# Fewer, wider idle matmuls between the stages, and H's tables loaded one page of x earlier

## The chip, the cores and the metric

The kernel runs on one core of a Trainium2 chip. The metric is the device time of one execution in microseconds (us). The kernel before takes 1393.24 us, the median of three runs (1391.94 to 1394.51).

## The reference

Three stages stand one behind the other. First the real part of a two-dimensional Fourier transform of x (8 x 3072 x 256), over the sequence and over the features. Then a mixture of experts with soft slots, and then a feed-forward layer with a squared rectifier:

```python
X = fft(fft(x, axis=1), axis=2).real.reshape(24576, 256)
logits = X @ phi                                  # 24576 x 32
d = exp(logits - logits.max(0)); d /= d.sum(0) + 1e-9
slot_input = (d.T @ X).reshape(8, 4, 256)
slot_out[e] = relu(slot_input[e] @ w1[e]) @ w2[e]  # e = 0..7
c = exp(logits - logits.max(1)); c /= c.sum(1) + 1e-9
Y = c @ slot_out
h = relu(Y @ w_in)
out = (s * h * h + b) @ w_out                      # 24576 x 256
```

## The kernel before, in words

The Fourier transform is never formed for all features. Because the logits are X @ phi, the features' transform is folded into phi (`project`, L480), and each batch of x is multiplied by that small matrix. The sequence of 3072 is split as 24 times 128.

**Stage V and T (to about 87 us).** 24 pages of x, 1 MB each, are loaded in turned form (`load_x`, L286). `emit_v` (L396) multiplies a part of a batch by the projected phi, `turn_v` transposes the result, and `emit_t` (L437) does the transform over 128 points into the table `tt`. The last batch is done in two pieces, `tpa` in a buffer with the tag "vq" and `tpb` in one with the tag "vt". Each tag has two buffers of PSUM, which the tiles take in turn. ScalarE copies `tpa` (L446) and VectorE copies `tpb` (L459) into `tt`.

**Logits (about 87 to 97 us).** The loop at L576 makes 16 blocks of logits, `lp` (L584), with 256 matmul instructions. ScalarE copies each into the pages `lg` (L597), and VectorE takes the maximum of each over its entries (L599). The maxima are joined into `cm1` (L606).

**The global maximum (to about 104.5 us).** `cm1` is transposed by TensorE (`mt`, L612), reduced by VectorE (L617), put on a diagonal (`dg`, L619), spread over all partitions by a product with ones (`mb`, L621), and copied to `cmb` (L622). Between the transpose and the reduction the program calls the remaining steps of the side work on the weights of the last layer (`side_step`, L614), which include VectorE's L216.

**H (to about 121 us).** The loop at L661 subtracts `cmb` from the logits (`emit_d`, on VectorE and POOL in turn, L647), takes exponentials on ScalarE (L683), and multiplies by the tables of H (L666). The two tables are loaded by `htab_load` (L349), which also clears parts of them on POOL. After the loads have landed, `htab_clear` (L358) moves and clears further parts on POOL.

**Sums, experts and last layer.** From 121 to about 180 us `r_sum` (L734) forms d.T @ x from 24 pages of x in a second layout (`load_xr`, L325), while the weights of the experts are loaded behind them. The experts follow. From about 230 us to the end the last layer runs; its matmuls (L1165, L1168, L1135) make up most of the time.

**Idle matmuls.** `keep_warm(t, k)` (L187) issues k matmuls of a matrix of ones into a PSUM tile that nobody reads. It is called ahead of `project` (L493), behind T (L533, four calls), and three times behind the logits (L610, L613, L624). A product of f32 operands is issued as two passes, so one call of `nc.tensor.matmul` gives two weight loads and two matmul instructions.

**What sets the order.** The instructions of each engine run in the order in which the program is written. All large loads are issued on SP's queue. While V runs, the letters of `ORDER` (L297) say which load comes next: x a page of x in turned form, w a part of w_out, s and l the tables of the logits, r a page of x in the second layout, h a table of H. `pump_a` takes the next letter when a page is free and the planner's clocks allow it, and L515 takes what is left. A load takes a page from a ring of 15. Pages of x that `ORDER` did not load are put at the head of the list `todo` (L564), whose entries are issued when pages come free.

Of the kernel before, what the change touches and what calls it, by code (L numbers as in the profile page):

```python
# [8 lines left out]
F32 = mybir.dt.float32  # L9
# [23 lines left out]
def tile_fft2__then__softmoe__then__act_relu2(  # L33
# [18 lines left out]
    nc = tc.nc  # L52
    P = 128
    NS1 = 24
    B, S, D = 8, NS1 * P, xp.shape[-1]
    NE = phi.shape[1]
    NG = B // 2
    M = 2 * NS1
    R = P // 2 + M
# [25 lines left out]
    ones = const.tile([P, P], F32, name="ones")  # L85
    dd = const.tile([P, 2, 2, D], F32, name="dd")
# [9 lines left out]
    def page(shape, dt, name, among=9):  # L96
        k = next(k for k, p in enumerate(pools[:among]) if p[2] < p[1])
        pools[k][2] += 1
        return pools[k][0].tile(shape, dt, tag="page", name=name), k
# [4 lines left out]
    def drop(k):  # L104
        pools[k][2] -= 1
# [5 lines left out]
    def dma_ready(cost=2.57):  # L111

        at["dma"] = max(at["dma"], at["pe"] - 1.0) + cost
        return at["dma"] + 1.3

    def busy(eng, cost, after=0.0):
        at[eng] = max(at[eng], after, at["pe"]) + cost
# [69 lines left out]
    def keep_warm(t, k):  # L187

        for _ in range(k):
            nc.tensor.matmul(t, lhsT=ones[:, :t.shape[0]], rhs=ones[:, :t.shape[1]], start=True, stop=True)  # L190

    def wo_load(k):
        if k % 2 == 0:
            t, kk = page([P, 8, D], F32, "wo")
            wo.append(t)
            wok.append(kk)
            whl.append(page([P, 8, 2, D], F16, "whl")[0])
        w = wo[k // 2][:, 4 * (k % 2):4 * (k % 2) + 4, :]
        hl = whl[k // 2][:, 4 * (k % 2):4 * (k % 2) + 4]
        d = w.rearrange("p k d -> p (k d)")  # L200
        top, inv = wsc[:, 0, 2 * k:2 * k + 2], wsc[:, 1, 2 * k:2 * k + 2]

        def scale():
            nc.vector.tensor_scalar(out=top, in0=top, scalar1=1e-30, scalar2=1.0 / WMAX, op0=ALU.max, op1=ALU.mult)
            nc.vector.reciprocal(inv, top)
            if k < 3:
                cast()

        def cast():
            for j in range(2):  # L210
                busy("act", 0.62)
                nc.scalar.activation(out=hl[:, 2 * j:2 * j + 2, 0, :], in_=w[:, 2 * j:2 * j + 2], func=AF.Copy,
                                     scale=inv[:, j:j + 1])

        def low(j):
            nc.vector.scalar_tensor_tensor(out=hl[:, 2 * j:2 * j + 2, 1, :], in0=w[:, 2 * j:2 * j + 2], scalar=inv[:, j:j + 1],  # L216
                                           in1=hl[:, 2 * j:2 * j + 2, 0, :], op0=ALU.mult, op1=ALU.subtract)
            if j and k % 2:
                drop(wok[k // 2])

        steps = double_steps(d, w_out.rearrange("(k p) d -> p k d", p=P)[:, 4 * k:4 * k + 4, :], False)
        steps.append((0.0, lambda: nc.vector.tensor_reduce(
            out=top, in_=d.rearrange("p (a n) -> p a n", a=2), axis=AX.X, op=ALU.max, apply_absolute_value=True), 1.15))
        steps.append((0.0, lambda: bias_add(k, d.rearrange("p (k d) -> p k d", d=D)), 0.0))
        steps.append((0.0, scale, 0.35))
        if k == 3:
            steps.append((0.0, cast, 0.0))
        steps += [(0.0, lambda j=j: low(j), 0.65) for j in range(2)]
        side_at[k] = dma_ready()
        side_work.extend((k, *f) for f in steps)  # L230
# [42 lines left out]
    def bias_add(k, d):  # L273

        for i in range(0 if k else 1, 4):
            nc.gpsimd.tensor_tensor(out=bias, in0=bias if k or i > 1 else d[:, 0], in1=d[:, i], op=ALU.add)
# [15 lines left out]

    NX = 3 * B
    CR = 1.5
    WARM = 4
    LEAD, TOL, LT, LX, HX = 14.0, 0.5, 0, 0, 1
    ORDER = "xxxwxxxxxxwxxxxxxwxxxxwxsrllrrrhh"  # L297
    tpool = tc.alloc_tile_pool(name="tpool", bufs=1)
    doubles += [((3, 1, 3, 1)[k], lambda k=k: wo_load(k)) for k in range(4)]

    order = list(ORDER)

# [78 lines left out]
    with tc.tile_pool(name="xtp", bufs=1, side="right") as xtp, tc.tile_pool(name="vp", bufs=1, side="right") as vp, \  # L381
# [108 lines left out]
                nc.vector.tensor_copy(phd[:, :, sg], pp.rearrange("p c j e -> p c (j e)"))  # L490
            nc.vector.tensor_scalar(out=phd[:, :, 1, NE:], in0=pp[:, :, 1], scalar1=-1.0, scalar2=None, op0=ALU.mult)

        keep_warm(psv.tile([P, 4 * P], F32, tag="vt", name="warm", bufs=2)[:, :P], 18)  # L493
        project()

        def step_v(n):
# [33 lines left out]
        side_step(0.0, True)  # L530
        nc.sync.dma_start(out=sb_in[:, 0:1], in_=sb_d[0].partition_broadcast(P))
        nc.sync.dma_start(out=sb_in[:, 1:2], in_=sb_d[1].partition_broadcast(P))
        keep_warm(psv.tile([P, 4 * P], F32, tag="vt", name="warm", bufs=2)[:, :P], WARM)  # L533
        for i in range(2):
            htab_clear(i)

# [35 lines left out]
    with tc.tile_pool(name="ps_l", bufs=6, space=PSUM) as psl, \  # L572
            tc.tile_pool(name="ps_m", bufs=1, space=PSUM) as psm:
        mxp[:] = [psm, 1]
        done_l = 0
        for st in range(NCH // 2):  # L576
            halves = [(h, (st + 4 * h) % 8) for h in range(2)]
            lps = {h: psl.tile([R, KC, NG * NE], F32, name="lp") for h, _ in halves}
            for k in range(2 * KC):
                q = P // 2 * (k % 2)  # L580
                m = M if q else P // 2
                for h, i8 in halves:
                    r = slice(64 * h, 64 * h + 64)
                    nc.tensor.matmul(  # L584
                        lps[h][q:q + m, k // 2, :], lhsT=ltabs[st // 4][0][r, 2 * KC * (i8 % 4) + k, 0:m],
                        rhs=tt[r, 2 * KC * i8 + k].rearrange("p b e -> p (b e)"), start=True, stop=True,
                        tile_position=(64 * h, q), skip_group_check=True,
                    )
            for h, i8 in halves:
                if h and st % 4 == 3:  # L590
                    drop(ltabs[st // 4][1])
                lp = lps[h]
                busy("dve", 0.55)
                at["pe"] += 1.06
                dst = lg[i8 // 2][:, 8 * (i8 % 2) + h:8 * (i8 % 2) + 8:2].rearrange("p k g e -> p k (g e)")
                if done_l < NCH - 1:
                    nc.scalar.copy(dst, lp)  # L597
                lv = lp.rearrange("p k (b e) -> p (k b) e", e=NE)
                nc.vector.tensor_reduce(out=cm[:, done_l, :], in_=lv.rearrange("p k e -> p e k"), axis=AX.X, op=ALU.max)  # L599
                if done_l == NCH - 1:  # L600
                    nc.scalar.copy(dst, lp)
                if done_l == NCH - 4:
                    nc.vector.tensor_reduce(out=cm[:, NCH, :], in_=cm[:, :NCH - 4, :].rearrange("p i e -> p e i"), axis=AX.X,
                                            op=ALU.max)
                if done_l == NCH - 1:
                    nc.vector.tensor_reduce(out=cm1, in_=cm[:, NCH - 4:, :].rearrange("p i e -> p e i"), axis=AX.X,  # L606
                                            op=ALU.max)
                done_l += 1
        warm = psl.tile([R, 2, B * NE], F32, name="lp")[:, 0, :R]
        keep_warm(warm, 8)  # L610
        mt = psm.tile([NE, R], F32, tag="mt", name="mt")
        nc.tensor.transpose(mt, cm1, ident[:R, :R])  # L612
        keep_warm(warm, 3)  # L613
        while side_step(0.0, True):  # L614
            pass
        cm2 = temps.tile([NE, 1], F32, name="cm2", bufs=1)
        nc.vector.tensor_reduce(out=cm2, in_=mt, axis=AX.X, op=ALU.max)  # L617
        dg = temps.tile([NE, NE], F32, name="dg", bufs=1)
        nc.vector.tensor_scalar(out=dg, in0=ident[:NE, :NE], scalar1=cm2, scalar2=None, op0=ALU.mult)  # L619
        mb = psm.tile([P, NE], F32, tag="mt", name="mb")  # L620
        nc.tensor.matmul(mb, lhsT=ones[:NE, :], rhs=dg, start=True, stop=True)  # L621
        nc.vector.tensor_copy(cmb, mb)  # L622
        mxp[0] = None
        keep_warm(warm, 8)  # L624
        fill_stack()

    temps.release()
# [10 lines left out]
    with tc.tile_pool(name="ps_h", bufs=3, space=PSUM) as psh:  # L638
# [22 lines left out]
        for i in range(-3, NCH + 1):  # L661
            if 0 <= i < NCH:
                dt = dts.pop(i)
                hp = [psh.tile([P, 2, 8 * MH], F32, name=f"hp{q}") for q in range(2)]
                for k, q in [(0, 0), (1, 0), (0, 1), (1, 1)] if i == NCH - 1 else [(0, 0), (0, 1), (1, 0), (1, 1)]:
                    nc.tensor.matmul(  # L666
                        hp[q][:, k, :], start=True, stop=True,
                        lhsT=dt.rearrange("p k g e -> p (k g e)")[:, 128 * (2 * k + q):128 * (2 * k + q) + 128],
                        rhs=htabs[i // 8][0][:, 2 * (i % 8) + k].rearrange("p q m -> p (q m)"),
# [231 lines left out]
    warm = pst.tile([P, 2, 2, P], F32, tag="htp_", name="warm")[:, 0, 0, :]  # L901
    sip = psa.tile([P, 2, NE], F32, tag="dps", name="sip")
    for c in range(2):
        for n, (j, k) in enumerate([(0, 0), (0, 1), (1, 0), (1, 1)]):
            nc.tensor.matmul(
                sip[:, c, :], lhsT=dd[:, j, k, c * P:(c + 1) * P], rhs=rt[:, k, 32 * j:32 * j + 32],
                start=(n == 0), stop=(n == 3),
# [144 lines left out]
    for _ in range(2):  # L1052
        p = pools.pop()
        assert p[2] == 0
        p[0].release()
    with tc.tile_pool(name="fr", bufs=4) as frp, tc.tile_pool(name="fo", bufs=3) as fo, \
# [134 lines left out]
        while len(seq) < 3 * NFC * NBLK:  # L1191
# [3 lines left out]
            t = min(may, key=lambda t: (done[t] + (t - 1) * lag, t))  # L1195
# [10 lines left out]
        for u, (n, f, t) in enumerate(seq):  # L1206
# [8 lines left out]
            if w % 6 == 3 and w < 36 and m % 4 == 3:  # L1215
                k = w // 6
# [107 lines left out]
```

## Time and profile before

| | us |
|---|---|
| median of three runs | 1393.24 |
| lowest and highest run | 1391.94, 1394.51 |
| the profiled execution's own time | 1392.02 |
| its span, first to last instruction | 1390.1 |
| TensorE busy, matmuls | 1370.7 |
| VectorE busy | 1169.2 |
| ScalarE busy | 1008.2 |

PE is TensorE, and PEld its weight loads, which run beside its matmuls. DVE is VectorE, ACT ScalarE, POOL GpSimd. SP issues transfers. A line such as L584 is a line of the kernel, and a line of a helper such as L190 stands for every call of it. In a chain of waits each piece is what the next one waited for; "issue" is time in which an engine waited for nothing that the profile shows. The queue "q1" carries the kernel's transfers, and "instruction" queues carry the engines' code.

### The profile page before, as it was taken

The numbers are of one execution on the slowest core, as the hardware profiler recorded it, in microseconds if no ns is written. First come the engines' busy times: TensorE is split into PE (matmuls) and PEld (weight loads), VectorE is DVE, ScalarE is ACT, GpSimd is POOL, SyncE is SP. The second block draws the span as 40 slices with busy tenths as digits, with TensorE's granted clock in tenths as the row PEclk, the third lists the DMA queues.
The fourth block names the chain that finished last, engine by engine and source line by source line (L and its number), as shares of the span: only waits on it lengthen the run. The fifth ranks groups of instructions, "written<-read, shape, count | busy, mean of one in ns | idle before, by whom it ended". The sixth has DMA issues, their size and how long they took to land.

```text
span 1390.1 us, 23074 instructions
## 1 busy us (share of the span) xinstructions
PE 1370.7 (99%) x9026; PEld 839.0 (60%) x9026; DVE 1169.2 (84%) x1490; ACT 1008.2 (73%) x1423; POOL 235.9 (17%) x286
## 2 busy tenths in 40 slices
PE   8989999999999999999999999999999999999998
PEld 6767555666666666666666666666666666666665
DVE  2577737998989898989898998989898989888886
ACT  2776126777778787777787777777777777777775
POOL 1057000121212121212121211111111111111110
PEclk9999999999999999999999999999999999999999
DMA  9997990101010101010102011010101010101000
GB/s 383 414 368 299 393 409 21 40 21 36 23 37 24 37 20 37 20 37 24 34 22 37 23 30 31 19 37 22 35 24 36 21 37 24 38 23 33 24 21 29
DMA packets 72733, 112.68 MB, mean 81 GB/s; under 512 B 34112, under 2 KB 59968, under 8 KB 65200
## 3 DMA queue, kind: packets, MB, share of 16 engines
q1 hardware_dynamic: 72592, 111.18, 23.7%
q8 instruction: 71, 1.16, 0.3%
q14 instruction: 38, 0.31, 0.1%
q0 software_dynamic: 32, 0.03, 0.0%
HBM read 78.89 MB, written 26.21 MB: 76 GB/s over the span
## 4 chain that ended last, share of the span: by engine, by line
PE 89%; DMA 2%; DVE 1%; issue 1%; ACT 0%; SPq 0%; DVEq 0%; ACTq 0%
PE op L1165 47%; PE op L1168 24%; PE fhp L1135 12%; PE racc L741 3%; DMA w2t<-in_moe_w_dram 2%; PE hp L666 1%; PE dps L726 1%; SPq L1098 0%; PE lp L190 0%; DVE cm L599 0%; DVE r L1141 0%; DVE rhl L1126 0%; PE eop L971 0%; PE lp L584 0%; PE gp L1069 0%
## 5 line engine op out<-in xcount | busy, mean ns | idle before, releaser
L1165 PE MATMUL op<-whl,rhl 128*128 128x512 f16 x3072 | 1025.3, 379 | 0.8 <-ACT rhl L1125 0.6
L1168 PE MATMUL op<-whl,rhl 128*128 128x256 f16 x3072 | 835.7, 273 | 0.0
L1140 ACT ACTIVATE r<-fhp,wsc 128x768 f32<-128x768 f32 (+1 forms) x513 | 461.9, 900 | 230.1 <-PE fhp L1135 229.1
L1141 DVE SCALAR_TENSOR_TENSOR r<-fhp,r 128x768 f32<-128x768 f32 (+1 forms) x513 | 488.6, 953 | 114.8 <-ACT r L1140 105.0
L1126 DVE TENSOR_TENSOR rhl<-r,rhl 128x768 f16<-128x768 f32 x511 | 505.5, 989 | 0.9 <-ACT rhl L1125 0.9
L1165 PEld LDWEIGHTS <-rhl 128*128 128x128 f16 x3072 | 300.5, 98 | 335.5 <-ACT rhl L1125 0.9
L1125 ACT CAST rhl<-r 128x768 f16<-128x768 f32 x511 | 420.0, 822 | 1.8 <-DVE r L1141 1.8
L1168 PEld LDWEIGHTS <-rhl 128*128 128x128 f16 x3072 | 300.6, 98 | 62.6 <-issue 0.3
L1180 POOL TENSOR_TENSOR ot<-ot,bias 128x256 f32<-128x256 f32 x189 | 138.9, 735 | 972.6 <-DVE ot L1178 972.6
L1135 PE MATMUL fhp<-ct,g 128*128 128x384 f16 x1024 | 250.4, 326 | 1.1 <-DMA g<-gs 0.9
L1135 PEld LDWEIGHTS <-g 128*128 128x128 f16 x1024 | 99.9, 98 | 69.0 <-issue 1.5
L1177 ACT ACTIVATE o<-op,small 128x256 f32<-128x256 f32 x189 | 90.0, 477 | 16.6 <-PE op L1168 16.6
L1178 DVE SCALAR_TENSOR_TENSOR ot<-op,small,o 128x256 f32<-128x256 f32 x192 | 91.5, 477 | 0.3
L408 PE MATMUL vt<-xb,phd 128*64 128x384 f32 (+3 forms) x288 | 48.7, 479 | 3.1 <-DMA xb<-in_x_turned_dram 2.7
L741 PE MATMUL racc<-xrt,dh 128*64 128x256 f32 x384 | 44.5, 383 | 0.4 <-DVE dh L731 0.4
L408 PEld LDWEIGHTS vt<-xb,phd 128*64 128x64 f32 x288 | 27.2, 139 | 21.9 <-issue 10.0
L741 PEld LDWEIGHTS racc<-xrt,dh 128*64 128x64 f32 x384 | 26.3, 137 | 20.9 <-issue 4.5
L478 ACT COPY tt<-tps 32x512 f32<-32x512 f32 x48 | 27.7, 577 | 5.1 <-PE tps L464 4.6
L420 ACT COPY vts<-vt 128x512 f32<-128x512 f32 (+1 forms) x16 | 8.5, 533 | 28.1 <-PE vt L408 27.9
L433 DVE COPY v<-vq 128x512 f32<-128x512 f32 (+1 forms) x15 | 8.3, 592 | 24.2 <-PE vq L429 24.2
L788 POOL TENSOR_TENSOR lg<-lg,rm 112x512 f32<-112x512 f32 x16 | 22.5, 1409 | 4.1 <-DVE rm L786 4.1
L770 POOL TENSOR_TENSOR lg<-et,lg 112x512 f16<-112x512 f32 x16 | 18.6, 1162 | 0.0
(228 smaller groups left out, 494.2 us busy)
## 6 DMA issues: line engine op xcount, KB each, us to landing
xb<-in_x_turned_dram SPq DMA_DIRECT2D x24, 1024.0 KB, 20.1
xrt<-in_x_pages_dram SPq DMA_DIRECT2D x24, 1024.0 KB, 12.5
out_dram<-ot SPq DMA_DIRECT2D x128, 128.0 KB, 1.7
w1t<-in_moe_w_dram SPq DMA_DIRECT2D x8, 1024.0 KB, 13.7
out_dram<-ot SPq DMA_DIRECT2D x128, 64.0 KB, 2.0
raw<-in_moe_w_out_dram SPq DMA_DIRECT2D x4, 1024.0 KB, 20.3
raw<-in_moe_w_in_dram SPq DMA_DIRECT2D x4, 1024.0 KB, 8.2
w2t<-in_moe_w_dram SPq DMA_DIRECT2D x4, 1024.0 KB, 17.9
```

What stands on the lines that cost most here:

```text
L408: nc.tensor.matmul(vt[64 * h:64 * h + 64, o:o + k, :], lhsT=phd[:, c, sg, :], rhs=turned(pg, c, i, k, rev), start=(c == 0 and m < 2), stop ...
L741: nc.tensor.matmul(raccs[acc][64 * h:64 * h + 64, :], lhsT=dh[:, m, g].rearrange("p j e -> p (j e)"), rhs=xr[k][0][:, g, t, :], start=(sum ...
L1125: nc.scalar.copy(a, r2)
L1126: nc.vector.tensor_tensor(out=l, in0=r2, in1=a, op=ALU.subtract)
L1135: nc.tensor.matmul(hp[k * split][:, k, :].rearrange("p (s b m) -> p s b m", s=2, b=B), lhsT=g16[:, f * P:(f + 1) * P], rhs=c, start=True, ...
L1140: nc.scalar.activation(out=r[:, k], in_=hp[i][:, k], func=AF.Relu, scale=wsc[:, 2, p:p + 1])
L1141: nc.vector.scalar_tensor_tensor(out=r2[:, k], in0=hp[i][:, k], scalar=0.0, in1=r[:, k], op0=ALU.max, op1=ALU.mult)
L1165: nc.tensor.matmul(op.rearrange("p h d -> p (h d)"), lhsT=a, rhs=w.rearrange("p h d -> p (h d)"), start=(f == 0), stop=False)
L1168: nc.tensor.matmul(op[:, 0, :], lhsT=l, rhs=w[:, 0, :], start=False, stop=(f == NFC - 1))
L1177: nc.scalar.activation(out=o1, in_=op[:, 1, :], func=AF.Copy, scale=qv)
L1178: nc.vector.scalar_tensor_tensor(out=ot, in0=op[:, 0, :], scalar=qv, in1=o1, op0=ALU.mult, op1=ALU.add)
L1180: nc.gpsimd.tensor_tensor(out=ot, in0=ot, in1=bias, op=ALU.add)
```

## The change

A new helper issues one product of n columns of the table dd instead of several of ones. The calls of `keep_warm` behind T and behind the logits are replaced by it: four calls of 128 columns become two of 512 in two tiles; 8, 3 and 8 calls of 112 columns become 3 of 512, 1 of 256 and 1 of 512. Ahead of `project` there are 16 calls in place of 18. In `ORDER` one of the letters r ahead of the tables of H is taken out; that page of x is issued from `todo` instead.

```diff
+    def keep_busy(t, n):
+
+        nc.tensor.matmul(t[:, 0:n], lhsT=ones[:, :t.shape[0]], rhs=dd[:, 0].rearrange("p k d -> p (k d)")[:, 0:n],
+                         start=True, stop=True)
+
-    WARM = 4
-    ORDER = "xxxwxxxxxxwxxxxxxwxxxxwxsrllrrrhh"
+    ORDER = "xxxwxxxxxxwxxxxxxwxxxxwxsrllrrhh"
-        keep_warm(psv.tile([P, 4 * P], F32, tag="vt", name="warm", bufs=2)[:, :P], 18)
+        keep_warm(psv.tile([P, 4 * P], F32, tag="vt", name="warm", bufs=2)[:, :P], 16)
-        keep_warm(psv.tile([P, 4 * P], F32, tag="vt", name="warm", bufs=2)[:, :P], WARM)
+        for _ in range(2):
+            keep_busy(psv.tile([P, 4 * P], F32, tag="vt", name="warm", bufs=2), 4 * P)
-        warm = psl.tile([R, 2, B * NE], F32, name="lp")[:, 0, :R]
-        keep_warm(warm, 8)
+        warm = psl.tile([R, 2 * B * NE], F32, name="lp")
+        for _ in range(3):
+            keep_busy(warm, 4 * P)
         mt = psm.tile([NE, R], F32, tag="mt", name="mt")
         nc.tensor.transpose(mt, cm1, ident[:R, :R])
-        keep_warm(warm, 3)
+        keep_busy(warm, 2 * P)
         while side_step(0.0, True):
             pass
...
         nc.vector.tensor_copy(cmb, mb)
         mxp[0] = None
-        keep_warm(warm, 8)
+        keep_busy(warm, 4 * P)
         fill_stack()
```

## Rows read from the trace of the kernel before

**Rows 1.** The page: busy time, share of the span, instructions of TensorE.

```profile
PE 1370.7 (99%) x9026; PEld 839.0 (60%) x9026; DVE 1169.2 (84%) x1490; ACT 1008.2 (73%) x1423; POOL 235.9 (17%) x286
```

**Rows 2.** The chain of waits, 84 to 110 us: start, duration, what.

```profile
91.97 0.62 issue
...
97.35 3.63 issue
...
103.71 0.56 PE mb L621 x2
...
106.54 0.25 issue
106.79 3.23 PE hp L666 x27
```

**Rows 3.** Stretches: length, busy (count) of PE PEld DVE ACT POOL, clock, transfers, GB/s.

```profile
87.13:91.97 4.84, 4.49 (x134) 3.68 (x130) 3.05 (x6) 4.74 (x10) 4.37 (x5) 1.00 1.04 408
92.58:97.36 4.78, 4.70 (x128) 4.10 (x128) 4.42 (x9) 3.61 (x7) 0.00 (x0) 1.00 0.83 197
```

**Rows 4.** Transfer queues in 87.2-89.9, 89.9-91.2, 91.2-98.3, 98.3-99.7 us: packets, MB, share.

```profile
q1 hardware_dynamic: 158, 1.16, 102.2%
...
q8 instruction: 1, 0.02, 4.9%
...
q1 hardware_dynamic: 555, 1.66, 91.3%
...
q8 instruction: 1, 0.02, 4.6%
```

**Rows 5.** Busy time by stretch, the granted clock behind the second gap.

```profile
102.40:105.80 3.40, 3.40 (x20) 3.14 (x20) 1.95 (x5) 0.55 (x2) 1.16 (x1) 0.58 1.03 419
```

**Rows 6.** The instructions in order of time, 24 to 33 us.

```profile
29.18 4.42 PE L408 MATMUL vt<-xb,phd 128*64 128x384 f32 x13 [2.70 <-DMA xb<-in_x_turned_dram]
```

**Rows 7.** The instructions in order of time, 66 to 108 us: the end of T.

```profile
84.29 1.16 PE L190 MATMUL warm<-ones 128*128 128x128 f32 x8
...
84.91 1.39 DVE L459 COPY tt<-tpb 64x512 f32<-64x512 f32 x2
...
86.97 3.12 PE L584 MATMUL lp<-tt,ltab 64*64 64x128 f32 x98 [1.52 <-ACT tt L446]
88.30 4.17 ACT L597 COPY lg<-lp 112x512 f32<-112x512 f32 x8
```

**Rows 8.** The chain of waits, 133 to 136 us: a product of 512 columns.

```profile
134.00 0.86 PE dps L726 x2
```

**Rows 9.** VectorE's instructions in order of time, 94 to 105 us.

```profile
94.15 3.08 DVE L599 TENSOR_REDUCE cm<-lp 112x32 f32<-112x512 f32 x5 [0.36 <-ACT lg L597]
...
99.77 0.43 DVE L606 TENSOR_REDUCE cm<-cm 112x32 f32<-112x160 f32 x1
100.11 1.41 DVE L216 SCALAR_TENSOR_TENSOR whl<-wo,wsc,whl 128x512 f16<-128x512 f32 x2
102.62 0.26 DVE L617 TENSOR_REDUCE cm<-mt 32x1 f32<-32x112 f32 x1 [1.11 <-PE mt L612]
102.92 0.23 DVE L619 TENSOR_SCALAR dg<-ident,cm 32x32 f32<-32x32 f32 x1
104.31 0.19 DVE L622 COPY cmb<-mb 128x32 f32<-128x32 f32 x1 [1.15 <-PE mb L621]
```

**Rows 10.** POOL's last work on H's tables, and ScalarE's first exponentials, in time order.

```profile
100.12 0.79 POOL L361 MEMSET htab_t<- 48x832 f32 x1
...
105.25 0.72 ACT L683 ACTIVATE dt<-dt 112x256 f32<-112x256 f32 x2 [4.01 <-DVE dt L647]
```

**Rows 11.** Busy time by stretch, 131 to 210 us; the chain at 180 us.

```profile
131.00:149.00 18.00, 18.00 (x142) 10.45 (x138) 13.15 (x22) 4.74 (x9) 8.45 (x9) 1.00 0.84 309
149.00:210.00 61.00, 60.44 (x564) 33.60 (x562) 31.95 (x49) 11.59 (x16) 1.26 (x2) 1.00 1.01 408
...
180.01 18.75 DMA w2t<-in_moe_w_dram
```

## The prediction

> **What bounds the kernel now.** The order of reading was: engine shares, stretches, chain, counts, transfers. TensorE is busy for nearly all of the span [rows 1], so only its gaps, and what it does needlessly, can be won; the edits touch the first 107 of 1390 us. The chain of waits from the logits to the first H product [rows 2] shows two gaps of TensorE marked "issue", which is waiting on nothing the profile shows: 0.62 us at 91.97 and 3.63 us at 97.35. H starts at 106.79.
>
> What the gaps are: between the end of the first (92.59) and the start of the second, TensorE ran 128 matmuls and 128 weight loads [rows 3], which is 256 instructions. Counting 256 back from 91.97 (the row has 264 with those under way at its edges) gives a point about 87.15, some 14 instructions into the logits. On the transfer side there is one packet of queue q8, 16 KB, in 89.9 to 91.2 and one in 98.3 to 99.7, and none in the stretches before each [rows 4]. So a block of 256 instructions of TensorE's code is asked for when the block before it is entered, and TensorE stops when it has used up one block before the next has come. From entry to resumption it took 92.59 - 87.15 = 5.4 us the first time and 97.35 + 3.63 - 92.59 = 8.4 us the second, with the transfer engines saturated. The logits use 256 instructions in under 5 us, so they outrun this.
>
> [...]
>
> [...]
>
> **The change part by part.** (a) Two warm-up calls fewer at the start. TensorE waits 2.70 us for a page of x at 29.18 [rows 6], and that page does not depend on TensorE. Whatever is won before it (two calls of four instructions, about 0.4 us) becomes a longer wait: nothing. Without that cover it would be 0.4 us gained. But 8 instructions leave the code.
>
> (b) Behind T: four narrow calls are 8 matmuls and as many loads, 16 instructions [rows 7]; two wide ones are 4 and 4. Together with (a), 16 instructions fewer lie ahead of the logits. A 512-column call in two passes costs 0.86 us of the chain [rows 8]. The first covers the time of the narrow ones. The second takes the other of the two "vt" buffers, which held tpb, so it must wait for VectorE's copies out of it, done at 84.91 + 1.39 = 86.30 [rows 7]. Behind it in TensorE's queue stand the logits, which waited until 86.97 for ScalarE. Now: 86.30 + 0.1 + 0.86 + 0.25 for the hand-over (the gap ahead of H after narrow calls [rows 2]) = 87.5, which is 0.55 late. Bounds: 0 if the buffer is free, 1.0 if the wide call runs at the lower clock. ScalarE takes its first logits only at 88.30, after other work [rows 7], so VectorE feels some 0.3.
>
> Where does the first stop fall now? 16 instructions further into the logits. At 98 matmuls and as many loads in 3.12 us [rows 7] that is 0.25 us of work. The block is entered at 87.15 + 0.55 + 0.25 = 87.95 and its successor is there 5.4 us later, at 93.4, against 92.59. TensorE is 0.8 late but 0.25 of work ahead, so the logits that VectorE waits for, 0.36 us until 94.15 [rows 9], come 0.55 late. From there VectorE is busy to 99.77 + 0.43 = 100.20, when the maxima cm1 stand [rows 9]. After: 100.75. Bounds: if the block comes early, that 0.36 of idle time is won against 0.3 lost by the late start, so 100.15; if it takes the 8.4 of the second time, resumption is at 96.35, 3.5 late, so 103.7.
>
> (c) Behind the logits. Before, 8 + 3 + 8 narrow calls, 76 instructions, and the second stop fell 12 instructions into them. Now it is 3 + 1 + 1 wide calls, 20 instructions, plus 6 for the two small products between: 26. The stop is 12 + 16 = 28 instructions behind the last logit, so it moves to H's first product. The block is asked for at 93.4 and even at 8.4 us is there at 101.8, before H can want it: the 3.63 us are gone, with about 3 us of cover. What is late next is VectorE, which works in order: after cm1 it still has the two L216 (100.11 to 101.52) before the maximum of mt [rows 9]. Before, the stop hid them; now they are on the path. So, from cm1: 1.32 to the end of L216; 0.04 + 0.53 for L617 and L619 (102.62 to 103.15); then the product mb. That took 1.15 before VectorE could copy it, partly behind narrow calls, partly at the lower clock; I take 0.6 (bounds 0.4 and 1.15), since the 0.56 of the chain [rows 2] at full clock and an empty queue should be less. Then 0.19 for the copy and, from its end at 104.50 to the exponentials' end at 105.25 + 0.72, 1.47 [rows 9, 10], and 0.2 to H's first load. Sum 4.35 us from cm1 to H. The wide calls end before they are needed: three take 2.6 us from about 97.2, until 99.8; the half call runs while VectorE works; the last, 0.86 us from about 103.3, ends before H at 105.1.
>
> H then starts at 100.75 + 4.35 = 105.1 instead of 106.79: 1.69 us gained. With cm1 at 100.15 it is 104.5, 2.3 gained; at 103.7 it is 108.05, 1.26 lost.
>
> (d) H's tables one page earlier. POOL cleared them until 100.12 + 0.79 = 100.91 [rows 10]; a page of 1 MB takes 2.5 us at 408 GB/s [rows 3], so it is done about 98.4. But POOL and H need that only when cmb stands, after 103, so nothing is won; were they four us later than before, it would cost. On SP's queue the moved page is issued behind two table loads and the two scalars; its first reader is the third step of the sums, after 124 us: nothing. POOL's memsets for the tables come earlier where it is idle.
>
> **Does it reach the end?** H and the sums are TensorE's; pages come free as it reads them, and from 131 to 149 the transfer engines still have room (0.84 busy) [rows 11]. From 149 to 210 they have none, and the chain at 180 runs over w2t. What they carry there is fixed, and the stretch starts when TensorE frees pages, so the whole shift passes on. Own time of the profiled run 1392.02 - 1.69 = 1390.3. The median is 1.22 above that run, so 1391.6 on its footing.
>
> **The rivals.** First: the first stop vanishes as well, because the block comes before it is wanted. For it: the tables, whose small packets slow the transfers (1.66 MB in the 7.1 us from 91.2 to 98.3 [rows 4], 234 GB/s), no longer stand in the way of the second block. Against: they move towards the first. Gain 2.3: 1390.9. Chance 0.2.
>
> Second, on the other side: the first stop becomes the long one. The tables now pass from about 88.5 on, just when the block that the logits need is asked for; with them in the queue the second block took 8.4 us. H at 108.05, 1.26 lost; a wait of 3.9 us also lets the clock fall, as the 3.63 did [rows 5], and 2.9 us at half speed cost up to 1.5, on the last logits and the idle matmuls behind them: 1394.5 to 1396. It decides from 7.1 us between entry and resumption (cm1 later than 102.44). Chance 0.15. [...]
>
> Third: the clock falls anyway. Between the wide calls and H TensorE does some 2 us in five, where the narrow calls filled all of it. H's first 2.9 us at half speed would cost up to 1.5: 1393.1. The gap of 1.52 us at 86.97 brought no fall. Chance 0.15.
>
> Fourth: the shift is given back at the transfers of w2t, because some release before 149 does not move. Against: TensorE has no long wait between H and there. 1393.2. Chance 0.1.
>
> **How the numbers follow.** The forecast has 0.4: 1391.6. Most cases lie within 0.2% (2.8 us, about what a measurement of this kernel can tell from no change), and medians of three scatter by about 1 us. Faster by more needs the first rival and some luck, or more than I see: 0.22. Slower by more needs the second with the clock and some scatter: 0.11. Within: 0.67. The range goes from the first rival with the scatter, 1389.2, to the second, 1395.2.
>
> **What would show it.** Right: no gap "issue" between the last logit and H; a gap near 92.4 that ends about 93.4; the logits' first matmul about 87.5 behind VectorE's L459; L617 directly behind L216; H at about 105; full clock from 85 to 120. Wrong: a gap of over 3 us within the logits, H later than 106.8, a clock fall in H, or w2t's last transfer still at 210.

## The result: 0.6% slower, and the profile after

The kernel after took 1406.23 us, the median of 12 executions (1391.8 to 1409.25), beside 1393.46 for twelve of the kernel before. The ratio, which goes by means, is 1.0062, with a 95% interval of 1.0039 to 1.0086; the medians are 0.9% apart. One execution of before, of 2322.2 us, stands alone and is left out of the ratio. The forecast was 1391.6, within 0.2%; the time lies outside its range.

The twelve executions fall in two groups. Five took 1391.8 to 1394.9 us at a mean granted clock of 0.996 to 0.999, and seven took 1406.2 to 1409.3 us at 0.985 to 0.988. The profiled execution (1406.28 us, span 1404.3) is of the second group. In the first the median is 1393.39, so even there the change shows no gain.

The engine shares of after. TensorE's busy time grew by 13.8 us although it has 36 instructions fewer [rows 1]:

```profile
PE 1384.5 (99%) x8990; PEld 848.7 (60%) x8990; DVE 1170.8 (83%) x1490; ACT 1008.5 (72%) x1423; POOL 233.5 (17%) x286
...
PEclk9995999999999999999999999999999999999999
```

The fourth slice of 35 us, 105 to 140, has the clock at 5 tenths of full speed. The chain of waits of after, 91 to 140 us and 196 to 227 us (start, duration, what), answers to [rows 2]:

```profile
91.98 3.08 issue
95.06 3.89 PE lp L589 x59
...
102.84 0.42 DVE cm L611
103.27 1.32 DVE whl L221 x2
104.59 0.18 DVE cm L623
...
105.08 0.42 PE mb L627 x2
...
107.31 27.63 PE hp L672 x128
...
215.05 9.94 DMA w2t<-in_moe_w_dram
225.03 1.93 PE eop L977 x26
```

There is one stop "issue" left, in the logits, of 3.08 us instead of 0.62. The second is gone: VectorE goes straight from L221 (L216 before) to the maximum of mt (L623). H starts at 107.31, 0.52 us later than before. But then H takes 27.63 us. In stretches of after (length, then busy time and count of PE, PEld, DVE, ACT, POOL, then clock, transfers, GB/s), [rows 5]:

```profile
95.84:99.25 3.41, 3.41 (x72) 3.41 (x68) 2.57 (x4) 2.37 (x5) 1.71 (x3) 0.50 1.02 423
...
102.70:107.30 4.60, 2.74 (x8) 0.85 (x7) 4.00 (x9) 2.19 (x9) 1.44 (x1) 0.87 1.02 424
107.30:134.90 27.60, 27.59 (x129) 27.60 (x130) 10.02 (x22) 13.47 (x31) 9.56 (x8) 0.50 0.44 175
```

and of before, for the same work:

```profile
101.88:105.29 3.41, 3.41 (x19) 3.11 (x18) 1.44 (x5) 0.04 (x1) 0.65 (x1) 0.50 1.02 420
106.79:121.27 14.48, 14.48 (x128) 14.34 (x128) 9.13 (x22) 12.36 (x31) 8.90 (x7) 1.00 0.83 343
```

The clock column, the granted share of full speed, is the reading. In before the clock fell after the second stop, at 101.88, and was back, at 105.29, before H. In after it fell twice ahead of H: behind the first stop, from 95.84 to 99.25 in the logits, and again at 106.08, out of a stretch in which TensorE worked 2.74 of 4.60 us. It came back at 136.8 only, although H kept TensorE busy for 27.59 of 27.60 us. H's median matmul takes 421 ns in after and 275 ns in before; the weight loads beside them are busy as long as H is (PEld 27.60).

The sum: H 0.52 later, H longer by 27.60 - 14.48 = 13.12 (by the stretches), and the rest, some 0.5, behind H; 0.3 of it lies in the transposes and products up to the first product of the sums. That is 14.2, the difference of the spans. It passes on whole: behind w2t the experts' first 26 products start at 225.03, against

```profile
210.89 1.93 PE eop L971 x26
```

in the chain of before.

### The profile page after: what moved, and what is told of

It reads as the page before. It is cut to its first block, busy times and chain, and to the rows that moved or that the text cites. A ratio compares the mean times of both kernels' runs of the same rounds, so it can differ in the third digit from the quotient of the medians.

```text
span 1404.3 us, 23001 instructions
## 1 busy us (share of the span) xinstructions
PE 1384.5 (99%) x8990; PEld 848.7 (60%) x8990; DVE 1170.8 (83%) x1490; ACT 1008.5 (72%) x1423; POOL 233.5 (17%) x286
## 4 chain that ended last, share of the span: by engine, by line
PE 89%; DMA 8%; DVE 1%; issue 1%; SPq 1%; ACT 0%; POOL 0%; DVEq 0%; POOLq 0%; ACTq 0%
PE op L1171 46%; PE op L1174 24%; PE fhp L1141 12%; DMA xb<-in_x_turned_dram 3%; PE racc L747 3%; DMA w2t<-in_moe_w_dram 2%; PE hp L672 2%; DMA raw<-in_moe_w_out_dram 1%; DMA lt<-in_ltab_dram 1%; PE dps L732 1%; SPq L1104 0%; DMA dd<-in_dft_d_dram 0%; DMA ltab<-lt 0%; PE lp L589 0%; DVE r L1147 0%
## 5 line engine op out<-in xcount | busy, mean ns | idle before, releaser
L1184 DVE SCALAR_TENSOR_TENSOR ot<-op,small,o 128x256 f32<-128x256 f32 x192 | 91.6, 477 | 0.3
L672 PEld LDWEIGHTS hp<-htab_t,dt 112*128 112x128 f32 x128 | 27.4, 333 | 1.6 <-issue 1.6
L672 PE MATMUL hp<-htab_t,dt 112*128 112x104 f32 x128 | 27.6, 422 | 0.4 <-ACT dt L689 0.4
```

The source lines that it names most:

```text
L672: nc.tensor.matmul(hp[q][:, k, :], start=True, stop=True, lhsT=dt.rearrange("p k g e -> p (k g e)")[:, 128 * (2 * k + q):128 * (2 * k + q) ...
L1184: nc.vector.scalar_tensor_tensor(out=ot, in0=op[:, 0, :], scalar=qv, in1=o1, op0=ALU.mult, op1=ALU.add)
```

## The experiments

Three theories of the fall were put to the test. Theory G: with fewer idle calls TensorE has too little to do (it is "thin") between the last logit and H, the clock falls, and H's own products don't lift it. Theory O: the new order of the loads is the cause, through the longer first stop. Theory W: wide calls hold the clock worse than narrow ones. "Low" below counts the executions with a mean clock under 0.99; each of them is 10 us or more above the others of its kernel. In e4's profile the clock comes back within H, at 113.17, and its six mean clocks are 0.992 to 0.998, so none is counted there, though all six are slower than before. First stop and start of H (its first product) are from the one profiled execution.

| run | order of loads | first stop | H starts | low | median us | ratio to before [95%] |
|---|---|---|---|---|---|---|
| after | new | 3.08 | 107.31 | 7 of 12 | 1406.23 | 1.0062 [1.0039, 1.0086] |
| e1 | old | 1.06 | 104.03 | 7 of 12 | 1404.2 | 1.0046 [1.0016, 1.0076] |
| e2 | new | 2.25 | 108.73 | 4 of 12 | 1396.88 | 1.0053 [1.0028, 1.0079] |
| e3 | new | 3.49 | 108.28 | 0 of 11 | 1394.03 | 1.0007 [0.9998, 1.0016] |
| e4 | new | 2.59 | 105.70 | 0 of 6 | 1402.75 | 1.0067 [1.0052, 1.0081] |
| e5 | old | 1.57 | 105.65 | 0 of 11 | 1391.14 | 0.9989 [0.9981, 0.9998] |
| e6 | new | 2.33 | 108.63 | 2 of 12 | 1393.27 | 1.0018 [0.9995, 1.004] |
| e7 | new | 2.84 | 106.54 | 0 of 11 | 1393.75 | 1.0009 [1.0000, 1.0018] |
| e8 | new | 4.29 | 108.50 | 0 of 11 | 1394.42 | 1.001 [1.0001, 1.0018] |
| e9 | old | 1.28 | 104.39 | 0 of 11 | 1390.69 | 0.9989 [0.9981, 0.9998] |
| e10 | old | 0.65 | 106.57 | 4 of 4 | 1405.9 | 1.0098 [1.0083, 1.0113] |

Ratios go by means, so where a kernel has two groups they are not those of the medians. e9 and e10 ran on another chip than e1 to e8, each beside before on its own. Of before's 90 other executions none is over 1395.02.

**e1, the order put back.** After, with the third r in `ORDER` again:

```diff
-    ORDER = "xxxwxxxxxxwxxxxxxwxxxxwxsrllrrhh"
+    ORDER = "xxxwxxxxxxwxxxxxxwxxxxwxsrllrrrhh"
```

> The changed kernel with one edit undone: three pages of x ahead of H's tables again. Theory G (the clock falls because TensorE has too little to do between the last logit and H, and H's own products don't lift it): no difference from the changed kernel, some executions near 1392 to 1395 and others near 1406 to 1409, these with a mean clock near 0.986. Theory O (the tables, now in the way of the code block, make the stop in the logits long, and that lets the clock fall): the stop at 92 shrinks from 3.1 to under 1 us and all executions lie at 1390 to 1395 with a clock of 0.996 or more. Theory W (wide idle matmuls hold the clock less well than narrow ones): as G.

Seven of twelve executions are still low (1403.4 to 1406.7), so O falls as the cause of the clock's fall. The other five took 1389.88 to 1391.63, about 2 us under before, where G had expected no difference from after's 1392 to 1395. The profiled execution (1390.31) is one of these. Its matmuls in order of time, and its stretches:

```profile
92.91 3.77 PE L589 MATMUL lp<-tt,ltab 64*48 64x128 f32 x114 [1.06 <-issue]
...
104.03 1.11 PE L672 MATMUL hp<-htab_t,dt 112*128 112x104 f32 x8 [0.46 <-ACT dt L689]
```

```profile
100.40:104.00 3.60, 2.12 (x7) 0.82 (x7) 3.03 (x7) 1.43 (x9) 1.09 (x1) 1.00 1.02 430
104.00:118.40 14.40, 14.18 (x125) 14.04 (x126) 10.80 (x22) 12.45 (x31) 10.08 (x8) 1.00 1.00 414
```

TensorE is as thin here (2.12 of 3.60 us), and the clock held in this execution, at 1.00. H takes 14.9 us, up to 118.97; behind its first eight products it waits for ScalarE's next exponentials. With the old order and a clock that holds, the idle calls bring H's start forward by 2.8 us and its end (121.30 in before) by 2.3.

**e2, narrow calls behind the logits.** After, with the old 8, 3 and 8 calls there; the wide ones behind T and the new order stay:

```diff
-        for _ in range(3):
-            keep_busy(warm, 4 * P)
+        keep_warm(warm[:, :R], 8)
-        keep_busy(warm, 2 * P)
+        keep_warm(warm[:, :R], 3)
-        keep_busy(warm, 4 * P)
+        keep_warm(warm[:, :R], 8)
```

> The changed kernel with 8, 3 and 8 narrow calls behind the logits again; the wide calls behind T, the 16 calls at the start and the order of loads stay. [...] O: the long stop stays, so executions near 1406 stay. [...] If H starts as in the changed kernel at 107.3, it may be up to 1 us later than before the change.

By G, with TensorE filled up to H again, none would be low and all would lie at 1391 to 1395, and by W too. Four of twelve are low. The matmuls of the profiled execution:

```profile
99.57 1.82 PE L190 MATMUL lp<-ones 128*112 128x112 f32 x16
102.98 0.27 PE L617 MATMUL mt<-ident,cm 112*32 112x112 f32 x1 [1.59 <-DVE cm L611]
103.08 0.75 PE L190 MATMUL lp<-ones 128*112 128x112 f32 x6
104.73 0.61 PE L626 MATMUL mb<-dg,ones 32*128 32x32 f32 x2 [0.90 <-DVE dg L624]
105.28 3.19 PE L190 MATMUL lp<-ones 128*112 128x112 f32 x16
108.73 3.45 PE L671 MATMUL hp<-htab_t,dt 112*128 112x104 f32 x29 [0.26 <-ACT dt L688]
```

There is no second stop in this kernel. The first eight narrow calls are over at 101.4, and TensorE waits 1.59 us for mt and 0.90 us for mb: narrow calls too leave it thin. The clock fell to 0.50 at 104.78 and was back at 108.20, ahead of H at 108.73, over the last eight calls. That in the four low executions it wasn't back in time is argued; none of them was profiled. W falls as the cause, since narrow calls lose the clock as well (4 of 12 against 7 of 12 can't tell which kind is worse). With the same nineteen calls before has 1.00 in all of H, so how many stand there isn't the point; by the reading at e6 it is when they run.

**e3, both gaps filled.** After, with wide calls added behind mt and behind mb:

```diff
         nc.tensor.transpose(mt, cm1, ident[:R, :R])
+        keep_busy(warm, 4 * P)
         keep_busy(warm, 2 * P)
...
-        keep_busy(warm, 4 * P)
+        for _ in range(2):
+            keep_busy(warm, 4 * P)
```

> The changed kernel with one more wide call behind the transposed maxima and one more behind the product with ones, so that TensorE is busy with wide calls nearly all the time from the last logit to H. G: no execution near 1406, all at 1391 to 1395, clock 0.995 or more. W: executions near 1406 stay, since it is the kind of call that does not hold the clock. O: they stay, too.

No execution of eleven is low, at a first stop of 3.49 us, longer than after's:

```profile
103.96:108.28 4.32, 3.87 (x11) 1.58 (x12) 3.75 (x7) 1.75 (x10) 1.78 (x2) 1.00 1.02 421
108.30:122.50 14.20, 14.20 (x127) 14.20 (x128) 9.45 (x22) 12.25 (x31) 9.24 (x7) 1.00 0.76 301
```

TensorE works 3.87 of the 4.32 us ahead of H, and the clock stands at 1.00 in H's 14.20 us. Its one fall between T and H, from 95.05 to 98.47 behind the first stop, was over within the logits. With the gaps filled the low executions are gone, at the order and the long stop that O blames: G's reading.

**e4, wide calls inside H.** After, with six wide calls into a buffer of the transposes, behind H's third block:

```diff
+                if i == 2:
+                    lift = pst.tile([P, 2, 2, P], F32, tag="htp_", name="lift").rearrange("p a b c -> p (a b c)")
+                    for _ in range(6):
+                        keep_busy(lift, 4 * P)
```

> The changed kernel with six wide idle calls put behind the third of H's sixteen blocks, and nothing else. [...]

By G the calls would lift the clock in H: the low executions would come to 1398 to 1402, and the others, which the calls only cost some 2.6 us, to 1394 to 1397. The six executions took 1398.6 to 1405.05, dearer than that, and none lies at 1394 to 1397. The profiled one (1401.09) in stretches:

```profile
105.70:110.50 4.80, 4.80 (x24) 4.67 (x25) 2.79 (x4) 3.26 (x8) 3.53 (x3) 0.57 1.02 418
110.50:113.10 2.60, 2.60 (x5) 1.08 (x4) 0.97 (x2) 0.70 (x2) 0.00 (x0) 0.50 1.01 416
113.20:117.00 3.80, 3.80 (x10) 1.67 (x9) 0.00 (x0) 0.00 (x0) 0.00 (x0) 1.00 0.71 293
117.00:129.40 12.40, 12.40 (x111) 12.24 (x110) 7.38 (x18) 9.12 (x23) 6.38 (x5) 1.00 0.26 87
```

The clock fell at 106.34, and H's products, busy throughout the first row, didn't lift it. Over the wide calls, 110.5 to 117, it rose, at 113.17, and the remaining 104 products ran at 1.00; in after no rise came within H (0.50 over 27.60 us). The other five have mean clocks of 0.992 to 0.997: (1 - 0.992) x 2 x 1400 = 22 us, down to 8 us, at 0.50 in the whole span, less than after's 36 and mostly more than the 7 of this one. What decides that is open.

**e5, filled and the order put back**: e3's edits and e1's.

> The changed kernel with two edits: the gaps filled as in e3 (one more wide call behind the transposed maxima, one more behind the product with ones), and three pages of x ahead of H's tables again as in e1. [...]

By G, with the new order only lengthening the first stop by some 2 us, H would start at 104 to 104.6 and all executions lie at 1390 to 1392.5. None is low, and the ratio is 0.9989 [0.9981, 0.9998]: faster than after, and than before by 0.1%, the interval just clear of 1. H started at 105.65, later than that, at a first stop of 1.57 us, and three of eleven executions lie above 1392.5, up to 1393.43.

**e6, the order alone.** Before, with only the new `ORDER`:

```diff
-    ORDER = "xxxwxxxxxxwxxxxxxwxxxxwxsrllrrrhh"
+    ORDER = "xxxwxxxxxxwxxxxxxwxxxxwxsrllrrhh"
```

> The kernel before with the new order of loads alone. Theory G: the narrow calls and the second stop stay, and the second stop hands the narrow calls to TensorE late, so that they run right up to H: no execution near 1406. The first stop grows from 0.6 to 2 to 3.5 us, and all executions move up by 1 to 2.5 us, to 1393.5 to 1396. Theory O in its strong form (the order makes the clock fall in H): executions near 1406 to 1410 appear.

The first stop is 2.33 us. Against expectation the second stop all but vanished; 0.24 us of it are left, in the loads of weights at 100.37. The second block's packet came little earlier (it started at 97.87, in before at 98.42), but TensorE came to the block's end 2.8 us later. Now the narrow calls behind the logits run at 99.46 instead of behind the stop, the gaps ahead of mt and mb are 1.27 and 0.90 us, and two of twelve executions are low (1407.07 and 1408.01), which none of the executions of before is:

```profile
94.17 5.36 PE L584 MATMUL lp<-tt,ltab 64*48 64x128 f32 x122 [2.33 <-issue]
99.46 2.14 PE L190 MATMUL lp<-ones 128*112 128x112 f32 x16
102.87 0.27 PE L612 MATMUL mt<-ident,cm 112*32 112x112 f32 x1 [1.27 <-DVE cm L606]
```

```profile
100.37 0.76 PEld L190 LDWEIGHTS lp<-ones 128*112 128x112 f32 x7 [0.24 <-issue]
```

The other ten have a median of 1393.02 against before's 1392.87, where 1393.5 to 1396 was expected: of a longer first stop their times show nothing.

So it was the second stop that sheltered before. Behind it the clock fell, at 101.88, but the stop also pushed the narrow calls (all but the first three) up against H, and over these the clock rose again, at 105.29. This reading rests on e2 and e6, the two kernels with the nineteen narrow calls and no such stop: 6 of their 24 executions are low, and none of before's 90. No run puts the stop back by itself.

**e7 and e8, one gap filled at a time.** After, with only e3's second edit (e7), or only its first (e8).

> The changed kernel with a second wide call behind the product with ones and nothing more behind the transposed maxima: of the two gaps only the one right ahead of H is filled. If that gap decides, no execution lies near 1406 and all are at 1392 to 1395.5 as in e3. If the gap behind the transposed maxima decides, 5 to 8 of 12 stay near 1406.

> The changed kernel with one more wide call behind the transposed maxima and nothing more behind the product with ones: the counterpart of e7. If the gap behind the maxima decides, all executions lie at 1392 to 1395.5. If the one ahead of H decides, 5 to 8 of 12 stay near 1406. If both share in it, each of the two kernels has some such executions, but fewer than the changed kernel's 7 of 12.

None of 11 is low in either, so in these executions one more wide call behind mt or behind mb is enough, and neither gap decides alone. Two executions of e7 (1397.34 and 1398.0) and two of e8 (1395.71 and 1396.08) lie above the expected range at a full clock; why isn't shown. With the new order both are no faster than before: 1.0009 [1.0000, 1.0018] and 1.001 [1.0001, 1.0018].

**e9, e8 with the old order.**

> The changed kernel with the old order of loads and one more wide call behind the transposed maxima, none more behind the product with ones: e5 without its last call. The call left out costs H's start about 0.6 us in e5, so if the clock holds, as it did in e8, all executions lie at 1389.5 to 1392, some 2 to 2.5 us under the kernel before. If the clock needs the last call as well, executions near 1404 to 1406 appear, since H now starts sooner behind a thinner stretch.

None is low; 1390.69 us, ratio 0.9989 [0.9981, 0.9998], with three of eleven above the expected 1392, up to 1393.25. Beside e5 it is the best version, with one call more than e1. Its matmuls:

```profile
93.27 3.77 PE L589 MATMUL lp<-tt,ltab 64*48 64x128 f32 x114 [1.28 <-issue]
...
104.39 1.11 PE L673 MATMUL hp<-htab_t,dt 112*128 112x104 f32 x8 [0.46 <-ACT dt L690]
```

```profile
100.70:104.40 3.70, 3.02 (x10) 1.25 (x10) 3.13 (x7) 1.53 (x9) 1.14 (x1) 1.00 1.00 423
```

Beside e1's 2.12 of 3.60 us TensorE works 3.02 of 3.70, and H starts only 0.36 us later.

**e10, no wide call at all, and the last narrow ones gone.** Before, without the eight calls behind mb:

```diff
         mxp[0] = None
-        keep_warm(warm, 8)
         fill_stack()
```

> The kernel before without its eight narrow calls behind the product with ones; all else as before, the order of loads too. Theory G: the second stop leaves TensorE idle from 97 to 101, and about 2 us ahead of H are now empty as well, so the clock falls in part of the executions and stays low through H: several of 12 at 1404 to 1408, the others at 1391 to 1394. Theory W (what counts is that wide calls took the place of narrow ones): no wide call is in it, so none near 1404.

All four executions are low, 1404.88 to 1406.88, where G had expected only several of twelve:

```profile
101.22 2.21 PE L190 MATMUL lp<-ones 128*112 128x112 f32 x10 [4.18 <-issue]
...
106.57 1.11 PE L665 MATMUL hp<-htab_t,dt 112*128 112x104 f32 x8 [1.50 <-ACT dt L682]
```

```profile
103.20:106.55 3.35, 1.87 (x11) 1.54 (x9) 1.90 (x5) 0.49 (x2) 1.11 (x1) 0.79 1.01 418
108.00:132.00 24.00, 24.00 (x114) 24.00 (x114) 9.23 (x20) 12.11 (x29) 8.45 (x7) 0.50 0.47 188
```

The clock fell behind the second stop, was back at 104.62 over the narrow calls, and fell again at 108.03, 1.5 us into H, behind a gap of 1.50 us; it stayed at 0.50 to 135.34. The loss of after is made here in the kernel before by taking calls away, at the old order and with narrow calls only. G stands as the cause; O and W don't.

## Why the prediction was wrong

**The step that failed** is the price of a fall of the clock. The sum that gives 1391.6 has no term for one; only the third rival has, "H's first 2.9 us at half speed would cost up to 1.5", at 0.15. Its 2.9 us are an estimate from the fall in before, (1 - 0.58) x 2 x 3.40 [rows 5]; the trace has 3.41 us at 0.50. But there narrow calls filled the time up to H, and over them the clock rose, at 105.29. Behind the change H itself follows, and in the profiled execution H doesn't lift it: the fall lasts through all of H, 0.50 over 27.60 us, and costs 13.12 us, nine times the term, and 7 of 12 executions are of this group. The third rival had the place right; with 13.12 in place of 1.5 its 1393.1 would have read 1404.7. The five executions without the fall, 1393.39 at the median, lie within the forecast range, if without the gain.

Being busy was not enough to bring the clock back here: over H's 27.59 busy of 27.60 us it stayed at 0.50, while over six wide calls in e4 it rose, at 113.17. What tells H's products from the others is not separated here.

**(b), the wide calls behind T**: the logits' first product was forecast at 87.5 behind VectorE's copies. It came at 86.76, 0.21 earlier than in before. The second wide call began at 85.28, while those copies ran on to 86.10, and the logits waited for ScalarE (L450) as they did before. The term of 0.55 was nothing.

**(b), the first stop**: right in its place, 16 instructions further on, wrong in its length. It ended at 95.06, between the forecast 93.4 and the 96.35 of the second rival. Behind it the clock was low from 95.84 to 99.25, on the last logits, as the second rival had it. So cm1 stands at 102.84 + 0.42 = 103.26 (forecast 100.75, second rival 103.7), later than the 102.44 from which that rival decides. The second rival and the third came in one execution; the prediction priced each alone. The first rival, in which this stop vanishes, is out.

**(d), the tables' move, costed at nothing**, is what lengthened it. In the profiles of the old order the first stop is 0.62 (before), 0.65, 1.06, 1.28 and 1.57 us; of the new one 2.25 to 4.29 in seven. They don't overlap. In time, with the clock at full speed and the wide calls in place, the new order costs the median of e3 against e5 2.9 us and of e8 against e9 3.7 us (taken in different sessions, the last pair on different chips; by their ratios to before, 0.0018 to 0.0021 of 1393, or 2.5 to 2.9 us), and the full-clock group of after against that of e1 1393.39 - 1390.72 = 2.7 us. That the stop belongs to the order is shown. The traces' packet records show where it arises: the 16 KB packet with the code is through at 90.9 to 92.3 us in the five profiles of the old order, at 92.7 to 95.0 in the seven of the new one, where in six it also takes 1.56 to 1.64 us itself instead of 1.0 to 1.1. In all twelve TensorE goes on 1.3 to 1.6 us behind it. Over all of before there are 71 such packets for 18052 matmuls and weight loads, one to 254, and behind its two stops the next one starts 5.83 us (98.42) and 3.60 us (104.58) after TensorE goes on. That fits the prediction's estimate, from [rows 3, 4], of a block asked for when the one before it is entered. Why it comes later under the new order is only argued: the tables' packets pass while the block of code is awaited. From 91.9 to 93.3 us the transfers of after are, beside [rows 4],

```profile
DMA packets 221, 0.18 MB, mean 129 GB/s; under 512 B 198, under 2 KB 198, under 8 KB 209
...
q8 instruction: 1, 0.02, 7.3%
```

198 of 221 packets under 512 bytes, in the stretch in which the block's packet came. In e1 that stretch, 90.2 to 91.6, has 9 of 81:

```profile
DMA packets 81, 0.58 MB, mean 411 GB/s; under 512 B 9, under 2 KB 9, under 8 KB 24
...
q8 instruction: 1, 0.02, 4.6%
```

With a wait of 5.4 us whatever passes, as the forecast had it, the stop would be the same under either order, and the seven profiles differ from that. No run separated the packets' size from their place.

**(c), the second stop**: gone, as forecast, with L623 directly behind L221. From cm1 to H it is 107.31 - 103.26 = 4.05 us, forecast 4.35. "The wide calls end before they are needed" was true of the three and the half call, and its cost was put at nothing: TensorE works 2.74 of 4.60 us ahead of H, and there the clock fell.

**Does the shift reach the end**: yes, 14.1 us at 225.03; and in e9, where H ends 2.0 us earlier than in before (119.33), the median is 1.9 lower. The fourth rival is out.

So a gain of the size forecast for (b) and (c) exists, 1.5 us by the ratio and 1.9 by the medians in e9, with one call more and the old order; but (d) takes it back, and the clock takes 13 more where it falls. Of the signs named as wrong, three came: a gap of over 3 us in the logits, H later than 106.8, and a clock fall in H.

## What to carry to other kernels

A fall of TensorE's clock is to be priced by the stage that follows, to its end, unless the trace shows that stage lift the clock: here H at 0.50, 27.60 us instead of 14.48; and since one kernel can run both ways, a dozen executions are to be looked at, not one profile. Before idle work is thinned, look at what runs directly ahead of such a stage: here one idle call of 512 columns, 0.4 us of delay to H (e9 against e1), decided over 13 us in 7 of 12 executions. By the reading at e6, before's stop of 3.63 us on code sheltered it by pushing idle work up to H, so removing such a stop has to be paired with putting that work there by hand.

## What the runs showed that was not expected

H's f32 products of 104 columns kept TensorE busy without a gap for 27.6 us (24.00 of 24.00 us in a stretch of e10) and stayed at 0.50 of full speed, while the clock rose within them over six idle calls of 512 columns in e4's profile. Behind the first stop of after the clock was back at 99.25, over the logits' products. One kernel ran in both ways, 7 and 5 of 12 executions, 15 us apart at the medians; what decides in a single execution was not found. A stop on TensorE's code grew from 0.62 to as much as 4.29 us when H's tables were loaded one page earlier, and that edit alone took a stop of 3.63 us at another place down to 0.24.
